# Row maxima of an attention kernel turned on VectorE and put in order through DRAM, in place of a product with the identity on TensorE

## The chip, the cores and the metric

The kernel runs on one core of one Trainium2 chip. The metric is the time of one execution on the device in microseconds (us), as the median of several runs; a time below the median before is faster. The profile comes from one further execution, which has its own time.

## The reference

The input x has 2048 rows of 512. Two attention layers of 32 heads with 16 dimensions each work on it, and a gate mixes them. A is full softmax attention over all 2048 keys. B cuts the rows into four segments of 512, takes causal softmax attention inside each segment, and adds what a running memory of the earlier segments gives.

```python
def _A_ref(x, wqkv, wo):
    ...
    scores = jnp.einsum("bhqd,bhkd->bhqk", q, k) * scale
    p = _softmax(scores, axis=-1)
    o = jnp.einsum("bhqk,bhkd->bhqd", p, v)
    ...
def _B_ref(x, wq, wk, wv, wo, beta):
    ...
    for s in range(N):
        ...
        logits = jnp.einsum("bhqd,bhkd->bhqk", qs, ks) * scale + mask
        p = _softmax(logits, axis=-1)
        a_dot = jnp.einsum("bhqk,bhkd->bhqd", p, vs)
        ...
        num = jnp.einsum("bhld,bhde->bhle", pq, M)
        den = jnp.einsum("bhld,bhd->bhl", pq, z)[..., None] + 1e-6
        o = g * (num / den) + (1.0 - g) * a_dot
        ...
g = _sigmoid((x * gate_w).sum(-1, keepdims=True))
return g * a + (1 - g) * b
```

What matters here is the softmax: the kernel needs the maximum of every row of scores before it can take the exponentials of that row.

## The kernel before

**Units and slots.** The work on the scores is cut into units. A unit is one side (A or B), one group g of four heads, and one chunk c of 512 queries. There are 32 units of each side, called k = 0 to 31 in the text (g = k mod 8, c = k div 8). An A unit has 64 slots and a B unit 10; a slot is one bank (128 x 512) of scores. The units follow each other as A0, B0, A1, B1, ..., A30, B30, B31, A31, so one k is 74 slots and there are 2368 slots, `nS`. The main loop counts them as `n`.

**Two passes.** Each score is computed twice. The pass for the maxima runs `LEAD` = 96 slots ahead, at position `m = n + LEAD`: TensorE makes scores with 128 queries in the partitions (`max_product`), and VectorE takes the maximum over the keys of each row, `tensor_reduce` for A, and `tensor_tensor_reduce` with the causal mask for B (`max_part`, `masked`). Four banks hold these scores; TensorE fills them in the order in which VectorE has read them. The first 96 positions run inside the projections (`some_max`). The second pass (`score_part`) makes the scores with the keys in the partitions, and here the maximum must already be subtracted: the query tile `qt[u]` has two further rows, 48 and 49 of each half, which hold the negated maximum in a high and a low part, and the key tiles have ones in these rows. ScalarE then takes the exponential straight from the bank (L805, L808), and TensorE multiplies by the values (`some_values`, L152 by way of the helper `matmul`).

**The order of the work.** It is written by hand. In a slot the jobs booked by `at` come first, then the score, then the part of the maxima, then `run_todo`. Slots come in bursts of three; at the end of a burst TensorE takes values, and in the last 94 slots (`wide`) in every second burst, along with pieces of the closing products (`fill`). `wait_early` puts the waits for loads of the next burst on the last product of the burst before. SyncE issues nearly all DMAs, in program order; a DMA that has to wait for something holds all that stand behind it. Keys and queries are loaded `PRE` = 20 slots ahead. `octet` divides a group of outputs by its sums of exponentials: GpSimd computes the factors, which go to DRAM and come back spread over the partitions; its jobs are booked at fixed distances, and it is put off where its factors would stand ahead of the maxima of a unit on GpSimd.

**The maxima on their way to the query tile.** The maxima of a unit lie as 128 partitions (queries of a block) x 16 (four heads, four blocks of queries). The score pass needs them as two rows of 2 x 512, one per half of the heads. So after the last maximum of a unit, `finish_max` reduces A's four values per row to one on VectorE (L204), and GpSimd splits the 16 columns into high and low part (L208, L209). Up to nine positions later (`LATE_T`) and at the end of a burst, `transpose_max` takes up to two units: TensorE multiplies each by the identity into a bank of the scores (L217), ScalarE copies the bank to `mt` (L220), and SyncE sends four pieces from there into the rows 48 and 49 of the query tiles (L223). A burst that does this does no `fill`.

Of the kernel before, what the change touches and what calls it, by code (L numbers as in the profile page):

```python
# [41 lines left out]
LATE_T = 9  # L42
# [5 lines left out]
def gated_mix(ctx, tc, x, xT, wqkv, a_wo, b_wq, b_wk, b_wv, b_wo, beta, gate_w, out):  # L48
# [88 lines left out]
    def raw(t):  # L137

        return t[:].bitcast(F32)
# [58 lines left out]
    late = []  # L198

    def finish_max(u):  # L200
        nm = pmt.pop(u)
        if u[0] == "A":
            pm, nm = nm, mp.tile([128, 4, 4], F32, tag="nm", name="nm")
            nc.vector.tensor_reduce(nm, pm, axis=AX.X, op=ALU.max, negate=True)  # L204

        ms = mp.tile([128, 2, 2, 2, 4], F32R, tag="ms", name="ms")
        nv = nm.rearrange("p (r h) s -> p r h s", r=2)
        nc.gpsimd.tensor_copy(ms[:, :, 0], nv)  # L208
        nc.gpsimd.tensor_sub(ms[:, :, 1], nv, ms[:, :, 0].bitcast(F32))  # L209
        return ms  # L210

    def transpose_max(us, pool, tag):

        w = 32 * len(us)
        pt = pool.tile([128, CH], F32, tag=tag, name="mt_ps")
        for i, (_, u, ms) in enumerate(us):
            nc.tensor.matmul(pt[32 * i:32 * i + 32, :128], ms.rearrange("p r a h s -> p (r a h s)").bitcast(F32), identf,  # L217
                             start=True, stop=True, tile_position=(0, 32 * i))
        mt = mp.tile([64, 128], F32R, tag="mt", name="mt")
        nc.scalar.copy(mt[:w], pt[:w, :128])  # L220
        for i, (_, u, ms) in enumerate(us):
            for r in range(2):
                lands["score", u, r] = [nc.sync.dma_start(raw(qt[u])[64 * r + 48:64 * r + 50],  # L223
                                                          raw(mt)[32 * i + 16 * r:32 * i + 16 * r + 16])]
# [23 lines left out]
    def max_part(m, bank, b=None):  # L248
# [3 lines left out]
        if u not in pmt:  # L252
            pmt[u] = mp.tile([128, 4, 4] + [4] * (side == "A"), F32, tag="pm" + side, name="pm")
# [29 lines left out]
        if m == last_max[u]:  # L283
            def finish():

                due = min(e for e in a_last if e >= last_max[u]) + LATE_T
                late.append((min(due, first[u] + LEAD - 12), u, finish_max(u)))
            todo.append((m + 1, finish))

    def run_todo(m):  # L290

        for e in [e for e in todo if e[0] <= m]:
            todo.remove(e)
            e[1]()
# [849 lines left out]
```

## Time and profile before

| | |
|---|---|
| median of 3 runs | 1768.63 us (1768.51 to 1768.84) |
| the profiled execution | 1769.23 us, of which its span is 1767.5 us |
| granted clock of TensorE | 1.00 |
| TensorE busy | 1760.7 us, 14873 products |
| VectorE busy | 1564.4 us, 3331 instructions |
| ScalarE busy | 1436.3 us, 2752 instructions |
| GpSimd busy | 641.0 us, 748 instructions |
| DMA | 261.54 MB, mean 148 GB/s |

The span runs from the first to the last instruction. In the rows PE is TensorE, PEld its weight loads, DVE VectorE, ACT ScalarE, POOL GpSimd and SPq the queue of SyncE; L260 is line 260 of the kernel before. The projections take the first 304 us or so, the main loop the rest. The ends of products are modelled, so that busy time of TensorE can hold waiting.

### The profile page before, as it was taken

How to read it: one execution, taken by the hardware profiler on the slowest of the kernel's cores; microseconds unless marked ns; L12 is line 12 of the kernel's file. 1: busy time of each engine (PE TensorE's matmuls, PEld its weight loads, DVE VectorE, ACT ScalarE, POOL GpSimd, SP SyncE). 2: the span in 40 equal slices, each digit the busy share in tenths (PEclk: the TensorE clock that was granted, in tenths of full speed). 3: DMA queues.
4: the chain of work that ended last, by engine and by line, in shares of the span. 5: the costliest groups of instructions: out<-in, count | busy, mean ns of one | idle time of the engine just before them, and what ended most of it. 6: DMA issues, size and time to landing. Idle time of an engine off the chain costs nothing.

```text
span 1767.5 us, 40472 instructions
## 1 busy us (share of the span) xinstructions
PE 1760.7 (100%) x14873; PEld 908.9 (51%) x14873; DVE 1564.4 (89%) x3331; ACT 1436.3 (81%) x2752; POOL 641.0 (36%) x748
## 2 busy tenths in 40 slices
PE   9999999999999999999999999999999999999999
PEld 8887776544444444444444444444444444444444
DVE  4235777999999999999999999999999999999931
ACT  5455444888888888888888888888889888888884
POOL 3002222415161416443434343343434253435343
PEclk9999999999999999999999999999999999999999
DMA  7677556444463436555444544454545444545542
GB/s 246 215 225 249 185 202 192 127 110 136 112 169 107 137 115 183 146 140 136 132 138 126 146 129 147 129 146 115 160 111 158 115 138 118 152 120 139 144 161 62
DMA packets 141269, 261.54 MB, mean 148 GB/s; under 512 B 36328, under 2 KB 58888, under 8 KB 140560
## 3 DMA queue, kind: packets, MB, share of 16 engines
q1 hardware_dynamic: 139712, 257.55, 50.3%
q8 instruction: 118, 1.93, 0.5%
q0 software_dynamic: 1216, 1.14, 0.3%
q14 instruction: 79, 0.65, 0.1%
q10 hardware_dynamic: 144, 0.26, 0.1%
HBM read 174.39 MB, written 83.25 MB: 146 GB/s over the span
## 4 chain that ended last, share of the span: by engine, by line
PE 96%; DVE 1%; ACT 1%; DMA 1%; POOL 1%; issue 0%; SPq 0%; POOLq 0%; ACTq 0%
PE ops L152 40%; PE st L785 27%; PE sm L227 14%; PE pr L352 10%; PE sm L152 2%; PE num L555 1%; POOL mn L419 1%; PE pr L442 1%; PE mps L586 0%; DMA qdB<-q 0%; PE mt_ps L217 0%; DMA raw<-xT 0%; PE sm L785 0%; DVE jk L514 0%; ACT ex L426 0%; DVE pm L260 0%
## 5 line engine op out<-in xcount | busy, mean ns | idle before, releaser
L808 ACT ACTIVATE p<-st 128x512 f32<-128x512 f32 x2261 | 1190.6, 601 | 146.7 <-PE sm L227 88.9
L260 DVE TENSOR_REDUCE pm<-sm 128x1 f32<-128x512 f32 x2048 | 1276.7, 680 | 11.3 <-PE sm L227 11.2
L227 PE MATMUL sm<-kA,qA 48*128 48x512 f32 x2048 | 664.1, 425 | 0.2
L785 PE MATMUL st<-qA,kA 50*128 50x512 f32 x2014 | 656.2, 431 | 0.0
L152 PE MATMUL ops<-p,vA 128*17 128x256 f32 (+3 forms) x6360 | 552.2, 445 | 0.0
L785 PEld LDWEIGHTS st<-qA,kA 50*128 50x128 f32 x2014 | 326.9, 185 | 423.0 <-ACT p L808 380.3
L227 PEld LDWEIGHTS sm<-kA,qA 48*128 48x128 f32 x2048 | 338.0, 185 | 13.1 <-issue 4.2
L904 POOL TENSOR_TENSOR rcp<-rec,minus 128x32 f32<-128x32 f32 x43 | 234.2, 5446 | 79.4 <-DMA rec<-dend 74.9
L275 DVE CUSTOM_DVE_ANT_0 rest<-sm,mask 128x128 f32<-128x128 f32 (+3 forms) x512 | 245.0, 479 | 0.0
L152 PEld LDWEIGHTS ops<-p,vA 128*17 128x17 f32 x6360 | 129.1, 96 | 213.0 <-issue 182.5
L789 POOL TENSOR_SCALAR_AFFINE_SELECT p<-p 128x512 f32<-128x512 f32 x128 | 79.4, 637 | 316.1 <-ACT p L808 311.4
L227 PE MATMUL sm<-kB,qB 48*128 48x128 f32 (+3 forms) x512 | 166.1, 384 | 0.0
L785 PE MATMUL st<-qB,kB 50*128 50x512 f32 (+1 forms) x495 | 105.5, 330 | 0.3 <-ACT mt L220 0.3
L422 DVE TENSOR_TENSOR q<-full,q 128x512 fp32r<-128x512 f32 x56 | 38.4, 688 | 75.5 <-ACT q L415 69.1
L785 PEld LDWEIGHTS st<-qB,kB 50*128 50x128 f32 x495 | 68.6, 186 | 62.0 <-ACT p L808 50.4
L152 PE MATMUL ops<-p,vB 128*17 128x128 f32 (+3 forms) x1504 | 88.4, 350 | 0.0
L227 PEld LDWEIGHTS sm<-kB,qB 48*128 48x128 f32 x512 | 80.0, 184 | 0.0
L208 POOL CAST ms<-nm 128x16 fp32r<-128x16 f32 x32 | 6.3, 196 | 196.7 <-DVE nm L204 194.9
L419 POOL TENSOR_SCALAR mn<-full 128x512 f32<-128x512 f32 x24 | 36.4, 1515 | 102.3 <-ACT full L414 81.9
L414 ACT COPY full<-pr 128x512 f32<-128x512 f32 x56 | 32.8, 587 | 41.1 <-PE pr L352 37.5
L208 POOL CAST ms<-pm 128x16 fp32r<-128x16 f32 x32 | 6.3, 196 | 128.7 <-DVE pm L275 128.6
L920 POOL TENSOR_TENSOR v<-v,inv 128x512 f32<-128x512 f32 x31 | 39.8, 1285 | 26.1 <-DMA inv<-rdA 22.5
(198 smaller groups left out, 1615.6 us busy)
## 6 DMA issues: line engine op xcount, KB each, us to landing
kA<-kdA SPq DMA_DIRECT2D x256, 128.0 KB
vA<-vdA SPq DMA_DIRECT2D x31, 544.0 KB
kA<-kdA SPq DMA_DIRECT2D x256, 64.0 KB
kdA<-q SPq DMA_DIRECT2D x32, 256.0 KB
qdB<-q SPq DMA_DIRECT2D x32, 256.0 KB
qA<-qdA SPq DMA_DIRECT2D x64, 128.0 KB
kdB<-q SPq DMA_DIRECT2D x32, 256.0 KB
qB<-qdB SPq DMA_DIRECT2D x64, 128.0 KB
```

The source lines that it names most:

```text
L152: behind[0] = nc.tensor.matmul(*args, **kw)
L227: nc.tensor.matmul(ps[:, n0:n0 + n], rows(qt[u][:, :, s * 128:(s + 1) * 128], h, 48), rows(k[:, :, k0:k0 + n], h, 48), start=True, stop=True)
L260: nc.vector.tensor_reduce(pm[:, h, s, kc:kc + 1], ps, axis=AX.X, op=ALU.max)
L275: nc.vector.tensor_tensor_reduce(out=tri["rest"][:, 0:w], in0=ps[:, n0:n0 + w], in1=tri["mask"][:, CH - w:], scale=-1.0, scalar=3.0e38, op ...
L352: nc.tensor.matmul(ps, l(a, k), r(b, k), start=(n == 0), stop=(n == 11))
L419: nc.gpsimd.tensor_scalar_min(ph["mn"], full, 0.0)
L422: nc.vector.tensor_sub(q2, full, q1.bitcast(F32))
L785: nc.tensor.matmul(ps[:, n0:n0 + CH - q0], rows(k[:, :, b * 128:(b + 1) * 128], h, 50), rows(q[:, :, q0:], h, 50), start=True, stop=True)
L789: nc.gpsimd.affine_select(out=x, in_=x, pattern=[[0, 4], [1, 128]], base=0, channel_multiplier=-1, compare_op=ALU.is_ge, fill=0.0)
L808: nc.scalar.activation(p[:, h], ps, AF.Exp, scale=SCALE)
L904: eng.tensor_tensor(r, rec, minus, op=ALU.pow)
L920: eng.tensor_mul(k["v"], k["v"], k["inv"])
```

## The change

The maxima of one A unit and one B unit share a tile. `couple` says which: A k goes with B k-1; A0 and B30 are alone, and A31 goes with B31. The tile `nm` has 128 partitions x 32 columns (two units, four heads, four blocks); B's masked maxima are written into it directly, and A's by the reduction as before. When both units of a tile are finished, `turn_max` has VectorE transpose the tile in 32-by-32 blocks, one position after that reduction; GpSimd splits the 32 columns into high and low part once. In the turned tile each block of 32 partitions holds 32 rows (unit, head, block of queries) of 32 queries, so that the pieces of one row lie in four places. SyncE puts them in order through DRAM: `keep_max`, four positions after the turn, stores the high and the low part in `sdm`, in pieces of 128 bytes; `send_max`, ten positions after the turn, loads two rows of 1024 into each half of both query tiles. The product, the copy by ScalarE, the bank, `LATE_T` and the lists `late` and `run_late` are gone; `fill` is no longer left out in any burst, and `octet` is put off by up to two positions more. A tile with one unit is cleared by GpSimd first.

```diff
--- before.py
+++ after.py
@@ -39,7 +39,7 @@
 LOW = 3
 NP = 6
 GAP = {"A": 2, "B": 5}
-LATE_T = 9
+SENT = 4, 10
 PRE = 20
 NKA, NKB = 8, 2
 
@@ -195,33 +195,59 @@
     pmt = {}
     tri = {}
     todo = []
-    late = []
-
-    def finish_max(u):
-        nm = pmt.pop(u)
+
+
+    couple = {}
+    for k in range(NU):
+        couple[unit("A", k)] = (k, 0)
+        if 0 < k < NU - 1:
+            couple[unit("B", k - 1)] = (k, 1)
+    couple[unit("B", NU - 2)] = (NU, 1)
+    couple[unit("B", NU - 1)] = (NU - 1, 1)
+    wanted = {}
+    for u, (k, _) in couple.items():
+        wanted.setdefault(k, set()).add(u)
+    nms = {}
+    sdm = [dr.tile([2, 2, 2, 8, CH // 4], F32, name=f"sdm{i}") for i in range(2)]
+
+    def nm_half(u):
+        k, i = couple[u]
+        if k not in nms:
+            nms[k] = mp.tile([128, 2, 4, 4], F32, tag="nm", name="nm")
+            if len(wanted[k]) == 1:
+                nc.gpsimd.memset(nms[k], 0.0)
+        return nms[k][:, i]
+
+    def finish_max(u, m):
         if u[0] == "A":
-            pm, nm = nm, mp.tile([128, 4, 4], F32, tag="nm", name="nm")
-            nc.vector.tensor_reduce(nm, pm, axis=AX.X, op=ALU.max, negate=True)
-
-        ms = mp.tile([128, 2, 2, 2, 4], F32R, tag="ms", name="ms")
-        nv = nm.rearrange("p (r h) s -> p r h s", r=2)
-        nc.gpsimd.tensor_copy(ms[:, :, 0], nv)
-        nc.gpsimd.tensor_sub(ms[:, :, 1], nv, ms[:, :, 0].bitcast(F32))
-        return ms
-
-    def transpose_max(us, pool, tag):
-
-        w = 32 * len(us)
-        pt = pool.tile([128, CH], F32, tag=tag, name="mt_ps")
-        for i, (_, u, ms) in enumerate(us):
-            nc.tensor.matmul(pt[32 * i:32 * i + 32, :128], ms.rearrange("p r a h s -> p (r a h s)").bitcast(F32), identf,
-                             start=True, stop=True, tile_position=(0, 32 * i))
-        mt = mp.tile([64, 128], F32R, tag="mt", name="mt")
-        nc.scalar.copy(mt[:w], pt[:w, :128])
-        for i, (_, u, ms) in enumerate(us):
-            for r in range(2):
-                lands["score", u, r] = [nc.sync.dma_start(raw(qt[u])[64 * r + 48:64 * r + 50],
-                                                          raw(mt)[32 * i + 16 * r:32 * i + 16 * r + 16])]
+            nc.vector.tensor_reduce(nm_half(u), pmt[u], axis=AX.X, op=ALU.max, negate=True)
+        del pmt[u]
+        k = couple[u][0]
+        wanted[k].remove(u)
+        if not wanted[k]:
+            todo.append((m + 2, lambda: turn_max(k, m + 2)))
+
+    def turn_max(k, m):
+
+        tt = mp.tile([128, 32], F32, tag="tt", name="tt")
+        nc.vector.transpose(tt, nms.pop(k).rearrange("p u h s -> p (u h s)"))
+        ms = mp.tile([128, 2, 32], F32R, tag="ms", name="ms")
+        nc.gpsimd.tensor_copy(ms[:, 0], tt)
+        nc.gpsimd.tensor_sub(ms[:, 1], tt, ms[:, 0].bitcast(F32))
+        sd = sdm[k % 2]
+
+        def keep_max():
+            for i in range(2):
+                nc.sync.dma_start(sd[i].rearrange("u r j (b q) -> b (u r j) q", b=4), raw(ms)[:, i])
+        todo.append((m + SENT[0], keep_max))
+        todo.append((m + SENT[1], lambda: send_max(k, sd)))
+
+    def send_max(k, sd):
+        for u, (k_, i) in couple.items():
+            if k_ == k:
+                for r in range(2):
+                    lands["score", u, r] = [nc.sync.dma_start(raw(qt[u])[64 * r + 48:64 * r + 50],
+                                                              sd[:, i, r].rearrange("a j q -> a (j q)"))]
 
     def max_product(ps, u, h, s, n0, n, k, k0=0):
         nc.tensor.matmul(ps[:, n0:n0 + n], rows(qt[u][:, :, s * 128:(s + 1) * 128], h, 48), rows(k[:, :, k0:k0 + n], h, 48),
@@ -250,7 +276,7 @@
         u, (r, i) = maxs[m]
         side, g, c = u
         if u not in pmt:
-            pmt[u] = mp.tile([128, 4, 4] + [4] * (side == "A"), F32, tag="pm" + side, name="pm")
+            pmt[u] = mp.tile([128, 4, 4, 4], F32, tag="pm", name="pm") if side == "A" else nm_half(u)
         pm = pmt[u]
         ps = bank()
         if side == "A":
@@ -281,23 +307,14 @@
                 rows_left.append(lambda h=h, s=s, n0=n0, w=w: masked(h, s, n0, w))
             rows_left.pop(0)()
         if m == last_max[u]:
-            def finish():
-
-                due = min(e for e in a_last if e >= last_max[u]) + LATE_T
-                late.append((min(due, first[u] + LEAD - 12), u, finish_max(u)))
-            todo.append((m + 1, finish))
+            todo.append((m + 1, lambda: finish_max(u, m)))
 
     def run_todo(m):
 
-        for e in [e for e in todo if e[0] <= m]:
-            todo.remove(e)
-            e[1]()
-
-    def run_late(pool, tag, m):
-        while us := [e for e in late if e[0] < m][:2]:
-            for e in us:
-                late.remove(e)
-            transpose_max(us, pool, tag)
+        while due := [e for e in todo if e[0] <= m]:
+            for e in due:
+                todo.remove(e)
+                e[1]()
 
     loaded = [0]
 
@@ -607,7 +624,6 @@
                 max_part(m + i, lambda: me_sm.tile([128, CH], F32, tag="sm", name="sm"))
             run_todo(m + 3)
             mnext[0] += 4
-            run_late(me_ps, "me", mnext[0])
 
         s0 = now[0]
         for n in range(5):
@@ -940,7 +956,7 @@
         ts = (0, 10, 14, 18, 28, 28) if ending else (0, 10, 18, 22, 32, 44) if (o, c) == (2, last) else (0, 10, 25, 29, 42, 54)
         if t0 is not None:
 
-            t0 += max([e + 2 - LEAD - t0 - ts[1] for e in a_last if 0 <= e + 1 - LEAD - t0 - ts[1] < 12], default=0)
+            t0 += max([e + 4 - LEAD - t0 - ts[1] for e in a_last if 0 <= e + 3 - LEAD - t0 - ts[1] < 12], default=0)
         for n, f in zip(ts, (load, factors, send, factor, scale, store)):
             if t0 is None:
                 f()
@@ -1084,15 +1100,11 @@
 
                 for i in range(4):
                     nc.tensor.matmul(ops[:, 128 * i:128 * i + 128], identf, identf, start=True, stop=True)
-            if any(e[0] < m + 1 for e in late):
-                run_late(st_ps, "st", m + 1)
-            else:
-
-                for _ in range(0 if n >= nS and queue else 4 if n not in wide else 11 - taken if taken < 8 else 0):
-                    if filled[0] == len(fill) or fill[filled[0]][0] > n:
-                        break
-                    fill[filled[0]][1]()
-                    filled[0] += 1
+            for _ in range(0 if n >= nS and queue else 4 if n not in wide else 11 - taken if taken < 8 else 0):
+                if filled[0] == len(fill) or fill[filled[0]][0] > n:
+                    break
+                fill[filled[0]][1]()
+                filled[0] += 1
             if 5 < n < nS:
                 wait_early(n)
         n += 1
```

## The prediction

> **What bounds the kernel now.** I read the page first (engine totals and the slices of the span), then the groups of VectorE for the long middle stage, then the busy time by stretches, then the order of time on VectorE, TensorE and SyncE around one turn of the maxima.
>
> ```profile
> span 1767.5 us, 40472 instructions
> ...
> PE 1760.7 (100%) x14873; PEld 908.9 (51%) x14873; DVE 1564.4 (89%) x3331; ACT 1436.3 (81%) x2752; POOL 641.0 (36%) x748
> ...
> DVE  4235777999999999999999999999999999999931
> ```
>
> By the page TensorE is the bound: 100% busy, 96% of the chain. But ends of matmuls are modelled, so a TensorE that waits for a bank can look busy. VectorE has only 89%, and its slices say why: low in the first seven slices and the last two, nine tenths or more in all the others. So the second view is VectorE alone from 305 to 1650 us, grouped (count | busy, mean ns | idle before).
>
> ```profile
> L260 DVE TENSOR_REDUCE pm<-sm 128x1 f32<-128x512 f32 x1904 | 1185.6, 680 | 0.0
> L275 DVE CUSTOM_DVE_ANT_0 rest<-sm,mask 128x128 f32<-128x128 f32 x480 | 229.6, 478 | 0.0
> ...
> L204 DVE TENSOR_REDUCE nm<-pm 128x16 f32<-128x64 f32 x30 | 6.2, 206 | 0.0
> ```
>
> No group has any idle time before it in 1345 us: VectorE works through the row maxima without a visible pause, and each k (one A unit and one B unit, 74 slots) takes what its maxima take. The stretches (TensorE, weight load, VectorE, ScalarE, GpSimd, then clock and DMA) show three k of that stage and the two stretches at the end:
>
> ```profile
> 614.69:750.25 135.56, 135.56 (x1277) 62.06 (x1278) 135.56 (x292) 120.98 (x235) 58.67 (x70) 1.00 0.54 150
> ...
> 1650.00:1705.00 55.00, 54.70 (x470) 25.19 (x458) 43.30 (x115) 47.74 (x95) 27.56 (x32) 1.00 0.38 112
> 1705.00:1767.00 62.00, 58.56 (x375) 31.32 (x373) 6.73 (x13) 38.79 (x78) 21.99 (x21) 1.00 0.38 123
> ```
>
> In the middle 135.56 of 135.56 us are VectorE's, while ScalarE has 14.6 us to spare. After 1650 VectorE runs out of maxima and TensorE (58.56 of the last 62.00) sets the end. Is VectorE really the one that is late in the middle, or do both run level? The order of time on VectorE answers (start, length):
>
> ```profile
> 592.82 9.49 DVE L260 TENSOR_REDUCE pm<-sm 128x1 f32<-128x512 f32 x15
> 602.22 0.21 DVE L204 TENSOR_REDUCE nm<-pm 128x16 f32<-128x64 f32 x1
> 602.35 3.07 DVE L260 TENSOR_REDUCE pm<-sm 128x1 f32<-128x512 f32 x5
> 605.34 0.28 DVE L275 CUSTOM_DVE_ANT_0 rest<-sm,mask 128x128 f32<-128x128 f32 x1
> ...
> 605.54 0.68 DVE L260 TENSOR_REDUCE pm<-sm 128x1 f32<-128x512 f32 x1
> 606.14 0.54 DVE L275 CUSTOM_DVE_ANT_0 rest<-sm,mask 128x384 f32<-128x384 f32 x1
> ...
> 606.62 0.68 DVE L260 TENSOR_REDUCE pm<-sm 128x1 f32<-128x512 f32 x1
> ```
>
> Five reductions from 602.35 to 605.34 are 0.598 us each, start to start, though each lasts 0.68: they overlap, and 0.60 is VectorE's own pace. The fifteen from 592.82 to 602.22 take 0.627: here TensorE is late, by 15 x 0.029 = 0.44 us. Another is seen 949 us on, 21 k later:
>
> ```profile
> 1541.65 9.49 DVE L260 TENSOR_REDUCE pm<-sm 128x1 f32<-128x512 f32 x15
> ```
>
> So TensorE is at times late, by some tenths of a microsecond in a k that takes 45.2; everywhere else VectorE is the bound, and only what is added to or taken from VectorE moves the end of the stage.
>
> **What is removed.** Per k, a pair of products with the identity on TensorE, a copy by ScalarE, one bank of the scores.
>
> ```profile
> 605.56 0.84 PE L152 MATMUL ops<-p,vA 128*17 128x128 f32 x16
> 606.23 0.39 PE L217 MATMUL mt_ps<-identf,ms 128*32 128x128 f32 x4
> 606.54 0.50 PE L785 MATMUL st<-qA,kA 50*128 50x512 f32 x1
> ...
> 607.50 0.84 PE L152 MATMUL ops<-p,vA 128*17 128x256 f32 x16
> 608.27 0.50 PE L785 MATMUL st<-qA,kA 50*128 50x512 f32 x1
> ```
>
> Without a turn the next scores start 0.77 us after such a group of values (607.50 to 608.27); with it 0.98 (605.56 to 606.54). So a turn costs TensorE 0.21 us. In the middle stage, which holds 30 of the 33, this is hidden: VectorE reduces on from its banks while TensorE does it, and the rows above show no gap at 606. I cost that removal at nothing there; if TensorE were the bound it would be 0.21 us each (rival below). The copy by ScalarE lies in ScalarE's spare time, and the bank likewise: nobody waits for them in the middle.
>
> Two places have no such cover. In the projections, where TensorE leads, and after the last maxima:
>
> ```profile
> 275.91 0.41 PE L217 MATMUL mt_ps<-identf,ms 128*32 128x128 f32 x2
> 276.25 1.13 PE L555 MATMUL num<-ph,mbd 128*128 128x512 f32 x2
> ```
> ```profile
> 1697.71 1.91 PE L152 MATMUL ops<-p,vA 128*17 128x512 f32 x16
> 1699.44 0.39 PE L217 MATMUL mt_ps<-identf,ms 128*32 128x128 f32 x4
> 1699.76 0.50 PE L785 MATMUL st<-qB,kB 50*128 50x512 f32 x2
> 1700.56 0.44 PE L785 MATMUL st<-qB,kB 50*128 50x384 f32 x1 [0.30 <-ACT mt L220]
> ```
>
> The first gives 276.25 - 275.91 = 0.34 us. The last turn takes 0.32 (1699.44 to 1699.76), and then the third score waits for the bank until the copy is done: the row shows 0.30 of it as idle. With the other late turn, taken at 0.21 as in the middle, the end gains 0.83 us. Bounds: nothing, if another wait ends last there, and 2.85 us (all of 1697.71 to 1700.56) at most. Taken: 0.34 + 0.83 = 1.2 us.
>
> **What is added on VectorE.** One turn of 128 x 32 per k: of 33 one falls into the projections, one (k = 31) behind the last maximum, and 31 into VectorE's full stage. The trace has no such instruction. Nearest rows: the masked pass over 128 columns takes 0.20 us to the next start (605.34 to 605.54), over 384 columns 0.48 (606.14 to 606.62): 0.0011 per column and 0.06 fixed. The 64-column reduction agrees (602.22 to 602.35, 0.13). [...] The lower bound is the fixed part alone, 0.06. The upper bound is the widest spacing of a small VectorE instruction that I find:
>
> ```profile
> 264.45 0.28 DVE L595 TENSOR_TENSOR mrun<-mps,mrun 128x136 f32<-128x136 f32 x1
> 264.77 0.46 DVE L596 SCALAR_TENSOR_TENSOR mbd<-mrun,gh,bmask 128x128 f32<-128x128 f32 x1
> ```
>
> 0.32 us, where the second waits for the first's result. The 64-column row is nearest, so 0.13: 31 x 0.13 = 4.0 us, with 31 x 0.06 = 1.9 and 31 x 0.32 = 9.9 as ends. The turn reads what the L204 reduction left one slot before; one maximum of 0.60 us lies between, so that result is there.
>
> [...]
>
> **GpSimd and SyncE.** GpSimd splits once per k instead of twice, 32 columns instead of 16.
>
> ```profile
> 602.50 0.20 POOL L208 CAST ms<-nm 128x16 fp32r<-128x16 f32 x1 [9.04 <-DVE nm L204]
> 602.77 0.22 POOL L209 TENSOR_TENSOR ms<-nm,ms 128x16 fp32r<-128x16 f32 x1
> ...
> 1655.94 0.64 POOL L789 TENSOR_SCALAR_AFFINE_SELECT p<-p 128x512 f32<-128x512 f32 x1 [12.74 <-ACT p L808]
> ```
>
> It waits for the maxima (9.04 us here), so it is there at once; behind its wait stand the factors of an octet, which the change moves two slots (1.2 us) back, with the loads and stores of that octet on SyncE, off the end's path. Two memsets are new, for the k with one unit; the second falls before 1655.94, into 12.74 us in which GpSimd only waits. Cost nothing, 0.3 us if VectorE had to wait for one.
>
> SyncE gets two stores and then loads that wait for both stores' landing; behind that wait are key loads, issued 20 slots (12 us) ahead. The old send was also waited for there. The B unit's first score is who would notice:
>
> ```profile
> 1243.65 0.37 SPq L913 DMA_DIRECT2D rdB<-rec  x1
> ...
> 1248.30 0.58 SPq L917 DMA_DIRECT2D inv<-rdB  x1
> ```
> ```profile
> 608.44 1.26 SPq L223 DMA_DIRECT2D qA<-mt  x2
> ```
> ```profile
> 613.73 0.49 PE L785 MATMUL st<-qA,kA 50*128 50x512 f32 x1
> 614.07 0.63 PE L785 MATMUL st<-qB,kB 50*128 50x512 f32 x2
> ```
>
> The store and load of the octet's factors, of the same shape, show a store's round trip of up to 4.65 us (1243.65 to 1248.30, SyncE waiting). For this k: turn at 602.95 (one maximum after L204), split done 603.8, second store issued about 604.0, landed by 608.65 at worst; then four loads, 0.63 us of issue each (608.44, two in 1.26) and A's ahead of B's, the last starting at 610.55. The rows must be there before 613.73. That leaves 3.2 us for the load to land, or 7.8 us for both landings. I cost it at nothing.
>
> [...]
>
> **The sum.** 4.0 - 1.2 = +2.8 us. The profiled execution took 1769.23 us (span 1767.5 and 1.7 around it) and becomes 1772.0; the median of the runs lies 0.6 lower, 1768.63, and becomes 1771.4.
>
> **Rivals.**
> - The turn does not overlap its neighbours on VectorE. Each reduction now starts the next 0.08 us before its own end (0.68 against 0.60); if reordering empties the pipe, a turn costs 0.2 to 0.32 us, 31 of them 6.2 to 9.9, the sum +5.0 to +8.7: 1773.6 to 1777.3, slower. It decides from 0.15 us a turn (31 x 0.15 - 1.2 = 3.5). For it: a reordering is unlike any row here. Against: every other form overlaps. [...]
> - The score rows come late: both landings over 7.8 us. TensorE then stands, VectorE lives an estimated 1.2 us on its filled banks (two maxima), and the rest is lost. With 4.65 us for each landing the rows are 1.5 us late, 0.3 lost in each of 30 k: 9 us on top of the 2.8, 1780.4 us, slower. For it: the round trip and A's loads ahead of B's. Against: a small load is read by one or two descriptors and the queues are half idle (0.54).
> - TensorE is the bound after all: then 30 x 0.21 = 6.3 us come back, with the 1.2: 1761.1, faster. For it: the page's 100% and the late stretches. Against: VectorE's even 0.598 and its idle 0.0.
> - The cheap end: 1.9 added, up to 3.2 won at both uncovered places: 1767.3.
>
> **How the numbers follow.** About 0.2% (3.5 us) is what a measurement here can tell from no change. Forecast with a turn of 0.09 to 0.15 us, 0.49 (all within 0.2%); cheap end 0.09 (within, but for 0.01 faster); no overlap 0.27; late rows 0.06; TensorE bound 0.09. So faster 0.10, same 0.57, slower 0.33. The range goes from the cheap end (1767.3, widened to 1767.0) to the dearest turn with only 0.5 us won: 1768.6 + 9.9 - 0.5 = 1778.0; TensorE as the bound and late rows, 0.15, are left out.
>
> **What would show it.** Right: VectorE's groups still have idle 0.0 from 305 to 1650, a new group of 31 turns with about 0.13 us to the next start, three k take 135.56 + 3 x 0.13 = 135.95 us; no row of TensorE waits for a load into qB; 275.91 and 1699.44 close up. Wrong: three k in less than 135.5 us (TensorE was the bound), spacing over 0.16, or scores of a B unit waiting for a DMA.

## The result: slower by 0.45%, inside the range and above the forecast

The kernel after takes 1777.16 us in the median (1772.88 to 1780.91, six runs) against 1768.81 (1768.51 to 1769.35); the ratio is 1.0045, 95% interval 1.0035 to 1.0055. That is +8.4 us where +2.8 was forecast. The runs also spread over 8.0 us, against 0.84 before. The execution that the profile shows is one of the short ones: 1775.33 us, +6.1 on the profiled execution of before.

The head of the page after:

```profile
span 1773.6 us, 40153 instructions
...
PE 1762.3 (99%) x14745; PEld 914.8 (52%) x14745; DVE 1567.9 (88%) x3364; ACT 1429.9 (81%) x2719; POOL 631.0 (36%) x688
```

TensorE is at 99% now. The turn itself is there as forecast. VectorE's groups from 305 to 1650 us, and the order of time around the turn of the k shown before:

```profile
L286 DVE TENSOR_REDUCE pm<-sm 128x1 f32<-128x512 f32 x1897 | 1183.2, 680 | 0.0
...
L233 DVE STREAM_TRANSPOSE tt<-nm 128x32 f32<-128x32 f32 x30 | 6.0, 199 | 0.0
```
```profile
602.32 0.21 DVE L223 TENSOR_REDUCE nm<-pm 128x16 f32<-128x64 f32 x1
602.44 0.68 DVE L286 TENSOR_REDUCE pm<-sm 128x1 f32<-128x512 f32 x1
603.04 0.20 DVE L233 STREAM_TRANSPOSE tt<-nm 128x32 f32<-128x32 f32 x1
603.16 2.44 DVE L286 TENSOR_REDUCE pm<-sm 128x1 f32<-128x512 f32 x4
```

The turn lasts 199 ns and the next reduction starts about 0.12 us after the turn's start (603.04 to 603.16); it overlaps its neighbours like the other forms around it. So the price of one turn, 0.13, was right. What was not forecast is in the waits of TensorE, 305 to 1670 us, and of VectorE, 305 to 1650 (total, times, longest):

```profile
PE ops L152 <- DMA qB<-sdm: 3.5, 2, 1.8
```
```profile
DVE rest L301 <- PE sm L253: 1.7, 1, 1.7
```

Twice TensorE stands until a load into qB has landed: B's score rows come late. The first time is at 705 us (the second falls behind 1650):

```profile
702.48 1.05 PE L152 MATMUL ops<-p,vA 128*17 128x384 f32 x14
705.25 0.38 PE L152 MATMUL ops<-p,vA 128*17 128x128 f32 x2 [1.72 <-DMA qB<-sdm]
```

SyncE's order of time shows why. First the k around 603 us, where the rows are in time, then the one that is late at 705 (its turn is at 693.28):

```profile
603.54 1.26 SPq L241 DMA_DIRECT2D sdm<-ms  x2
606.26 0.53 SPq L249 DMA_DIRECT2D qA<-sdm  x2
606.85 0.54 SPq L249 DMA_DIRECT2D qB<-sdm  x2
```
```profile
693.37 0.53 SPq L186 DMA_DIRECT2D kA<-kdA  x1
...
696.34 0.47 SPq L754 DMA_DIRECT2D vA<-vdA  x1
697.15 1.30 SPq L241 DMA_DIRECT2D sdm<-ms  x2
702.62 0.56 SPq L249 DMA_DIRECT2D qA<-sdm  x2
703.23 0.54 SPq L249 DMA_DIRECT2D qB<-sdm  x2
```

At 603 the stores go out half a microsecond after the turn, and the loads follow 2.7 us behind (603.54 to 606.26). At 697 seven loads are issued first (from 693.37 to 696.34, keys, output blocks and values), and then the stores take 5.5 us until the loads may go (697.15 to 702.62), because they travel behind those big loads: in the trace the packets of the blocks and values move from 696.6 to 701.4 and the 128-byte pieces of the stores from 700.6 to 702.0. The load into qB is issued at 703.23 and lands two microseconds later, at 705.2.

The second late row, at 1657.81, is late mainly in the queue. Its turn is at 1645.94, but two of B's key loads stand ahead of the stores and wait, one 2.1 us for the blocks to land, the other 2.4 us for the values:

```profile
1651.84 0.30 SPq L187 DMA_DIRECT2D kB<-kdB  x1
1652.24 1.59 SPq L241 DMA_DIRECT2D sdm<-ms  x2
1655.29 0.53 SPq L249 DMA_DIRECT2D qA<-sdm  x2
```

Here the loads follow the stores after only 3.1 us. From the turn to the first load it is 9.3 us in both late k. A long landing alone does no harm: in the k whose turn is at 1102.60 the stores leave at 1103.11, the loads follow 5.9 us behind them, and no row is late.

How much of the 6.1 us is what? A mark that returns in every k is A's last reduction; from its row in k = 1 to its row in k = 30 are 29 k. Before, then after:

```profile
331.14 0.21 DVE L204 TENSOR_REDUCE nm<-pm 128x16 f32<-128x64 f32 x1
...
1641.19 0.21 DVE L204 TENSOR_REDUCE nm<-pm 128x16 f32<-128x64 f32 x1
```
```profile
330.71 0.20 DVE L223 TENSOR_REDUCE nm<-pm 128x16 f32<-128x64 f32 x1
...
1645.21 0.21 DVE L223 TENSOR_REDUCE nm<-pm 128x16 f32<-128x64 f32 x1
```

The 29 k take 1310.05 before and 1314.50 after, 4.45 more. One of them, the late one, took 47.50 us where the others of its kind take 45.54: 1.96. The other 2.5 are the turns, 0.09 in each k. The last k, with the second late row, is 2.05 longer (53.85 for 51.80). The stage starts 0.43 earlier (331.14 to 330.71). 4.45 + 2.05 - 0.43 = 6.07, and the end, which was to gain 0.83, gives nothing. The rows of the end that answer to 1697.71, 1699.76 and 1700.56 of before:

```profile
1703.56 1.91 PE L152 MATMUL ops<-p,vA 128*17 128x512 f32 x16
1705.40 0.68 PE L801 MATMUL st<-qB,kB 50*128 50x512 f32 x3
1705.74 0.34 PE L801 MATMUL sm<-qB,kB 50*128 50x384 f32 x1
```

From the values to the score that had to wait for the bank, it is 2.18 us now and was 2.85: 0.67 are won here, of which 0.4 are left at the next product of values (1701.28 before, 1706.72 after). The other late turn gives 0.2, so that TensorE gains 0.6 in all. It is lost at the very end. ScalarE's last copy of the result, before and after:

```profile
1763.60 0.58 ACT L1107 COPY res<-sm 128x512 f32<-128x512 f32 x1 [0.72 <-PE sm L152]
```
```profile
1769.02 0.58 ACT L1119 COPY res<-sm 128x512 f32<-128x512 f32 x1 [0.72 <-PE sm L152]
```

From there to the end of the span are 3.9 us before (1767.5 - 1763.60) and 4.6 after (1773.6 - 1769.02): what stands behind the last copy took 0.7 longer. It isn't the landing of the last stores: in the trace SyncE's last wait for one ends at 1766.6 before and at 1771.9 after, 0.9 and 1.7 us from the end, so that the 0.7 lie in the program's closing instructions. In the kernels below the stretch from the last copy is 3.8 to 4.3 us; such a difference of one profile each is taken as scatter. In the kernel below that has no product it is 3.9 as before, and there the 0.6 is seen: from the last maximum to the end it is 74.5 us, for 75.1 before.

### The profile page after: what moved, and what is told of

It is laid out like the page before. It is cut to its first block, busy times and chain, and to the rows that moved or that the text cites. A ratio compares the mean times of both kernels' runs of the same rounds, so it can differ in the third digit from the quotient of the medians.

```text
span 1773.6 us, 40153 instructions
## 1 busy us (share of the span) xinstructions
PE 1762.3 (99%) x14745; PEld 914.8 (52%) x14745; DVE 1567.9 (88%) x3364; ACT 1429.9 (81%) x2719; POOL 631.0 (36%) x688
## 3 DMA queue, kind: packets, MB, share of 16 engines
q0 software_dynamic: 1216, 1.14, 0.3%
## 4 chain that ended last, share of the span: by engine, by line
PE 92%; DMA 3%; DVE 1%; ACT 1%; POOL 1%; issue 0%; SPq 0%; POOLq 0%; ACTq 0%; DVEq 0%
PE ops L152 39%; PE st L801 26%; PE sm L253 14%; PE pr L369 9%; PE sm L152 2%; POOL mn L436 1%; PE pr L459 1%; PE num L572 1%; DVE pm L286 1%; DMA vA<-vdA 0%; DMA qdB<-q 0%; DMA kA<-kdA 0%; ACT full L431 0%; DMA sdm<-ms 0%; PE sm L801 0%
## 5 line engine op out<-in xcount | busy, mean ns | idle before, releaser
L253 PE MATMUL sm<-kA,qA 48*128 48x512 f32 x2048 | 672.7, 428 | 0.3
L235 POOL CAST ms<-tt 128x32 fp32r<-128x32 f32 x33 | 6.9, 210 | 234.8 <-DVE tt L233 234.7
L152 PEld LDWEIGHTS ops<-p,vB 128*17 128x17 f32 x1504 | 33.6, 96 | 27.9 <-issue 24.2
```

The costliest lines, as they stand in the source:

```text
L152: behind[0] = nc.tensor.matmul(*args, **kw)
L253: nc.tensor.matmul(ps[:, n0:n0 + n], rows(qt[u][:, :, s * 128:(s + 1) * 128], h, 48), rows(k[:, :, k0:k0 + n], h, 48), start=True, stop=True)
```

## The experiments

The theory behind the forecast was that VectorE alone is the bound in the middle, so that a turn there costs its 0.125 us, TensorE's relief nothing, and SyncE and GpSimd nothing. The rivals: TensorE is (also) the bound, and the score rows come late through SyncE's queue and the two trips through DRAM. For each kernel the time of the 29 k is read as above; where GpSimd does A's last reduction, from the reductions behind it, which serve as marks in the same way. Two more stretches are named below: the projections, from A1's first reduction to A2's first (64.16 us before, 64.05 after), which holds their end, and the last k, from A30's last reduction to the end of A31's last (51.80 before).

**The turn alone.** The kernel before, with one turn of a constant tile per k on VectorE.

```diff
+    blank = const.tile([128, 32], F32, name="blank")
+    nc.gpsimd.memset(blank, 0.0)
+
+    def dead_turn():
+        tt = mp.tile([128, 32], F32, tag="tt", name="tt")
+        nc.vector.transpose(tt, blank)
...
             todo.append((m + 1, finish))
+            if u[0] == "A":
+                todo.append((m + 2, dead_turn))
```

> The kernel before, with one more VectorE instruction per k: a transpose of a constant 128 x 32 tile one position after A's last reduction, whose result nobody reads. Products, copies and sends stay. Theory (VectorE is the bound of the middle stage, a turn costs 0.125 us to the next start): 30 turns in the full stage, +3.8 us, about 1772.5, with no spread between runs. Rival (the turn itself is free or hidden, and all that the change lost it lost in waits for the score rows): 1768.7, within 0.5 us of the kernel before. Rival (a turn empties the pipe): +6 or more.

Measured: 1771.7 us (1770.68 to 1772.59), ratio 1.0014 (1.0006 to 1.0023), +2.9 us.

```profile
331.60 0.21 DVE L210 TENSOR_REDUCE nm<-pm 128x16 f32<-128x64 f32 x1
...
1644.45 0.21 DVE L210 TENSOR_REDUCE nm<-pm 128x16 f32<-128x64 f32 x1
```

1312.85, which is 2.80 over before and 0.097 per k: about three quarters of a turn's 0.125 stay. That is the forecast's main term, by itself. The runs lie within 1.9 us, so the turn makes neither the rest of the loss nor the spread.

**The product twice.** The kernel before, with both products with the identity done a second time.

```diff
-        for i, (_, u, ms) in enumerate(us):
+        for i, (_, u, ms) in [e for e in enumerate(us) for _ in range(2)]:
```

> The kernel before, with every product that turns the maxima done twice into the same bank (the second overwrites the first). Theory (TensorE's 0.21 us per turn is hidden behind VectorE in the middle stage): only the places without that cover show it, +0.3 in the projections and at most 0.6 at the end, so under +1 us. Rival (TensorE is as much the bound as VectorE): 30 x 0.2 = +6 us and more.

Measured: 1775.18 us, ratio 1.0034 (1.0022 to 1.0047), +6.3 us. The expectation failed.

```profile
330.20 0.21 DVE L204 TENSOR_REDUCE nm<-pm 128x16 f32<-128x64 f32 x1
...
1645.88 0.21 DVE L204 TENSOR_REDUCE nm<-pm 128x16 f32<-128x64 f32 x1
```

1315.68: 5.63 more, 0.19 per k. The second pair takes 0.24 us of TensorE (from the values to the scores it is now 1.22 us, for 0.98 before), so four fifths of it stay. TensorE has next to no margin in the middle.

**No product.** The kernel before without product, copy and bank: the rows are sent straight from ms, in the wrong order.

```diff
-        pt = pool.tile([128, CH], F32, tag=tag, name="mt_ps")
...
-        nc.scalar.copy(mt[:w], pt[:w, :128])
...
-                                  raw(mt)[32 * i + 16 * r:32 * i + 16 * r + 16])]
+                                  ms.rearrange("p r a h s -> p (r a h s)").bitcast(F32)[64 * r:64 * r + 64])]
```

> The kernel before without the product, the copy by ScalarE and the bank: the rows 48 and 49 are filled straight from the split maxima, in the wrong order, by the same number of sends at the same places; no turn on VectorE and no way through DRAM. It shows what the removal alone is worth. Theory: the two places without cover, 0.4 in the projections and 0 to 0.8 at the end, so 1767.5 to 1768.4. Rival (TensorE the bound): 1761 to 1762.

Measured: 1768.21 us, ratio 0.9996 (0.9987 to 1.0004). The 29 k take 1310.08, as before (1310.05). So taking 0.21 away gives nothing, though adding 0.24 costs most of it.

**A's last reduction on GpSimd.** The kernel before, with 0.125 us per k taken from VectorE.

```diff
-            nc.vector.tensor_reduce(nm, pm, axis=AX.X, op=ALU.max, negate=True)
+            d = mp.tile([128, 4, 4, 3], F32, tag="d", name="d")
+
+            def larger(out, a, b):
+                nc.gpsimd.tensor_sub(out, a, b)
+                nc.gpsimd.tensor_scalar_max(out, out, 0.0)
+                nc.gpsimd.tensor_add(out, out, b)
+            larger(d[:, :, :, 0:2], pm[:, :, :, 0:2], pm[:, :, :, 2:4])
+            larger(d[:, :, :, 2:3], d[:, :, :, 0:1], d[:, :, :, 1:2])
+            nc.gpsimd.tensor_scalar_mul(nm, d[:, :, :, 2], -1.0)
```

> The kernel before with A's last reduction (four values per row to one, 0.126 us on VectorE per k) made by seven small GpSimd instructions instead, as b + max(a - b, 0) twice and a change of sign. Theory (VectorE is the bound): 30 x 0.126 = -3.8 us, about 1765.0, since GpSimd has some 9 us of waiting ahead of these maxima and the product that needs them comes up to nine positions later. Rival (both engines run level, so that taking from VectorE alone gives nothing): 1768.7. Rival (the later split delays the product or the sends): slower.

Measured: 1768.25 us, ratio 0.9997 (0.9988 to 1.0006). The expectation failed: the 29 k take 1309.55, half a microsecond less, where VectorE as the only bound had to give 29 x 0.125 = 3.6. Two of every three k became shorter by 0.08 (44.96 to 44.88, 45.10 to 45.03), the third longer by 0.13 (45.46 to 45.59); why the third grows isn't shown.

**Both at once.** The two last edits together (the rows in the wrong order again).

> The kernel before with both removals at once: no product, copy and bank (rows sent straight from the split maxima, in the wrong order), and A's last reduction on GpSimd. Alone each gave -0.6 us. Theory (VectorE and TensorE run level, so that what is taken from one is waited for at the other): together more than the sum, in the middle stage some 0.1 us per k, about 1765.5. Rival (VectorE alone is the bound and some third thing limits it): the sum of the two, 1767.6.

Measured: 1765.13 us, ratio 0.9973 (0.9962 to 0.9983), -4.3 us.

```profile
328.77 2.49 DVE L261 TENSOR_REDUCE pm<-sm 128x1 f32<-128x512 f32 x4
...
1635.85 2.48 DVE L261 TENSOR_REDUCE pm<-sm 128x1 f32<-128x512 f32 x4
```

1307.08: 2.97 less, where the two edits alone gave 0.0 and 0.5. So the two engines run level in the middle. To take from one alone gives next to nothing, because the other is right behind; to add to either costs most of what is added; to take from both pays.

**Rows without the round trip.** The kernel after, its stores kept, but the rows loaded from a DRAM tile that is filled once, so that no load waits for a store (the rows are not the maxima then).

```diff
+    fixed = dr.tile([2, 2, 2, 8, CH // 4], F32, name="fixed")
...
-        todo.append((m + SENT[1], lambda: send_max(k, sd)))
+        todo.append((m + SENT[1], lambda: send_max(k, fixed)))
```

> The changed kernel with its stores as they are, but with the rows loaded from another DRAM tile that is filled once at the start, so that no load waits for the landing of a store (the rows are not the maxima). Theory: SyncE no longer stands between store and load, 2.2 to 5 us are gone from the way, and no row is late: about 1771.5. Rival (SyncE's backlog of issues ahead of the stores, or the loads' own landing, makes the rows late): waits for qB remain, over 1773.

Measured: 1771.22 us (1770.51 to 1772.40), ratio 1.0009 (1.0000 to 1.0018). No wait for qB is left, the 29 k take 1312.79, and the time is that of the turn alone. What the change costs beyond its turn, and its spread, hangs on the load's wait for the store.

**Everything as early as it can be.** The kernel after with no slots of delay before the stores and loads, and B's rows ahead of A's.

```diff
-SENT = 4, 10
+SENT = 0, 0
...
-        for u, (k_, i) in couple.items():
+        for u, (k_, i) in reversed(couple.items()):
```

> The changed kernel with the two stores and the loads of the rows right behind the turn in SyncE's order (SENT 0, 0 in place of 4, 10), so ahead of the value tile (544 KB) and the blocks (512 KB) that are issued one slot later, and with B's rows ahead of A's. Theory (the changed kernel's cost above the turn's 2.9 us comes from rows of B that land late, because their stores and loads stand behind those big loads): no wait of TensorE for a load into qB, little spread, about 1771.5. Rival (the way through DRAM is late by itself, whatever stands ahead): waits as before, 1774 to 1780. Rival (SyncE, held earlier at the landing of the stores, delays other loads): slower than the changed kernel, with TensorE waiting for keys or values.

Measured: 1782.05 us, ratio 1.0068 (1.0055 to 1.0080), slower still. In the 29 k no row is late (1312.86, as with the turn alone), but the projections got 5.8 us longer (69.85 for 64.05), and the last k 6.6 (58.5 for 51.9). In the last k SyncE is held at the new stores (5.3 us, until GpSimd's split is done), and a key load behind them comes late. TensorE's waits from 1650 us on, and the stretches around (in the order of the prediction's), the first of them in the projections:

```profile
PE ops L152 <- DMA kB<-kdB: 3.2, 1, 3.2
```
```profile
282.70:289.50 6.80, 6.80 (x13) 4.14 (x14) 4.74 (x11) 1.08 (x2) 0.00 (x0) 0.50 0.91 202
...
1664.00:1668.00 4.00, 2.55 (x9) 1.17 (x9) 0.13 (x1) 0.35 (x1) 0.00 (x0) 0.64 0.39 121
1668.00:1670.00 2.00, 2.00 (x12) 0.15 (x8) 1.93 (x6) 1.27 (x3) 0.65 (x1) 0.50 0.00 0
1670.00:1672.00 2.00, 2.00 (x14) 1.46 (x10) 0.56 (x3) 1.36 (x3) 0.00 (x0) 0.51 0.02 7
1672.00:1674.00 2.00, 2.00 (x16) 1.38 (x14) 1.96 (x7) 1.30 (x3) 0.00 (x0) 1.00 0.36 132
```

The stall of 3.2 us is followed by a granted clock of about one half until 1672, which loses another 4 x 0.36 + 2 x 0.50 + 2 x 0.49 = 3.4 us. With the 3.2 that is the 6.6 of the last k: this stall cost twice what its wait shows. In the projections the clock is one half for 6.8 us as well, which is 3.4 of the 5.8.

**Stores from GpSimd.** The kernel after with the stores issued by GpSimd right behind its split, loads as they were.

```diff
-SENT = 4, 10
+SENT = 0, 10
...
-                nc.sync.dma_start(sd[i].rearrange("u r j (b q) -> b (u r j) q", b=4), raw(ms)[:, i])
+                nc.gpsimd.dma_start(sd[i].rearrange("u r j (b q) -> b (u r j) q", b=4), raw(ms)[:, i])
```

> The changed kernel with the two stores issued by GpSimd, right behind its split, on its own queue; the loads stay on SyncE ten positions after the turn. Theory (the stores are late because of SyncE's order and the one queue): GpSimd issues them about 1 us after the turn, SyncE finds them landed, no late rows: 1771.5 to 1772.5. Rival (GpSimd's queue takes longer to land, or its issue holds back the factors behind it): more late rows, or GpSimd's pow later, 1775 and more.

Measured: 1773.7 us (1772.78 to 1775.71), ratio 1.0023 (1.0015 to 1.0032).

TensorE's wait for qB, and SyncE's from 516 to 525 us:

```profile
PE ops L152 <- DMA qB<-sdm: 1.2, 1, 1.2
```
```profile
SPq L249 <- DMA sdm<-ms: 7.1, 1, 7.1
```

Two k are still late, by less (46.02 for 45.05, and 53.2 for 51.9 in the last; the wait shown is that of the last), and the projections take 2.6 us longer, of which 1.7 are a granted clock of one half from 276.9 to 280.3. Half a cure: the store leaves early, but that doesn't make it land early. In the first of the two k the stores are issued at 515.87, 0.2 us after a load of values, and SyncE stands 7.1 us at the loads until they have landed. In the last k the loads stand behind the waiting key loads, as in the kernel after, and then wait 2.9 us more.

**Early only where nothing is in the way.** The kernel after with no delay for 0 < k < 30 and the old delays elsewhere, and with B's rows first in every k.

```diff
+        sent = (0, 0) if 0 < k < 30 else SENT
...
-        for u, (k_, i) in couple.items():
+        for u, (k_, i) in reversed(couple.items()):
```

> The kernel after, with the stores and loads of the score rows both put ahead of the big key and value loads (no slots of delay, B's rows first) for every k of the middle stage, and left where they were in the two k whose early store stood in the way of loads (the first one, in the projections, and the last ones). If the late rows of B and SyncE's stand behind a store are what the change costs beyond its turn, no k of the middle has a late row, and the time falls from 1777 us to that of the dead turn alone, 1771.7, plus at most 1.9 for the late row that k = 30 keeps: 1771.5 to 1773.5. If the excess came from something else that the new turn brings (GpSimd's one long split, the missing score bank, the moved octet factors), it stays at 1775 or above.

Measured: 1771.11 us (1770.48 to 1772.48), ratio 1.0012 (1.0004 to 1.0021). No wait for qB or for keys up to 1670 us.

```profile
330.54 0.20 DVE L223 TENSOR_REDUCE nm<-pm 128x16 f32<-128x64 f32 x1
...
1643.19 0.20 DVE L223 TENSOR_REDUCE nm<-pm 128x16 f32<-128x64 f32 x1
```

1312.65, again the time of the turn alone. All that it changes is the place of six DMAs in SyncE's queue. So the loss of the change is settled in two parts: 2 to 3 us for the turn, and the rest for late rows. In k = 30, where the old delays stand, this profile has no late row either: the stores leave 3.4 us after their turn (1643.91 to 1647.26) instead of 6.3, because the key loads ahead of them waited less. How much of that is owed to the edit isn't shown.

**The same, with A's last reduction on GpSimd.** The turn comes three slots later, and VectorE's work per k is that of the kernel before again.

```diff
-            nc.vector.tensor_reduce(nm_half(u), pmt[u], axis=AX.X, op=ALU.max, negate=True)
...
+            nc.gpsimd.tensor_scalar_mul(nm_half(u), d[:, :, :, 2], -1.0)
...
-            todo.append((m + 2, lambda: turn_max(k, m + 2)))
+            todo.append((m + 5, lambda: turn_max(k, m + 5)))
```

> As the kernel before it in this list, and A's last reduction (64 columns, 0.125 us on VectorE) done by GpSimd in seven short operations, the turn three slots later. VectorE then has the same work per k as in the kernel before (a turn for a reduction), and TensorE 0.21 us less. If both engines run level, the middle stage is that of the kernel before or 0.1 us per k shorter, and the time 1766 to 1770 us. If VectorE had margin for the turn and only late rows counted, the time is that of the list's first kernel, 1771.5 to 1773.5.

Measured: 1858.0 us, ratio 1.0499 (1.0484 to 1.0513); neither expectation. TensorE's waits, and GpSimd's order of time in one late k:

```profile
PE ops L152 <- DMA qB<-sdm: 46.5, 13, 5.6
```
```profile
424.88 0.27 POOL L231 TENSOR_SCALAR nm<-d 128x16 f32<-128x16 f32 x1
425.10 5.46 POOL L929 TENSOR_TENSOR rcp<-rec,minus 128x32 f32<-128x32 f32 x1
...
432.30 0.21 POOL L243 CAST ms<-tt 128x32 fp32r<-128x32 f32 x1
```

Between the reduction and the split, GpSimd now has an octet's reciprocal, 5.46 us, and five more steps of it; the split comes 7.2 us after the reduction. The edit had moved the split past the slots that the change keeps free of octets.

The 13 stalls are 46.5 us of the 89 that are lost. After 11 of them the granted clock was one half, for 3.4 or 6.8 us each, which loses another 27. Whether it falls isn't settled by the length of the stall alone: behind two stalls of 1.9 us, which end at 825.37 and at 1399.12, are these stretches:

```profile
825.50:829.00 3.50, 3.50 (x25) 1.39 (x23) 2.11 (x7) 2.15 (x5) 0.00 (x0) 1.00 0.77 260
...
1400.80:1404.20 3.40, 3.40 (x18) 1.36 (x16) 2.26 (x7) 2.43 (x5) 0.00 (x0) 0.50 0.43 115
```

**The octets put off.** The last kernel, with every octet step within six slots of A's last maximum behind the turn.

```diff
-            t0 += max([e + 4 - LEAD - t0 - ts[1] for e in a_last if 0 <= e + 3 - LEAD - t0 - ts[1] < 12], default=0)
+            t0 += max([e + 7 - LEAD - t0 - ts[1] for e in a_last if 0 <= e + 6 - LEAD - t0 - ts[1] < 12], default=0)
...
+        if n < nS - 90 and any(0 <= n + LEAD - e < 6 for e in a_last):
+            beside[n + 1] = beside.pop(n, []) + beside.get(n + 1, [])
```

> The kernel with the early rows and A's last reduction on GpSimd, once more, now with every step of an octet that falls within six slots after A's last maximum put off behind the turn on GpSimd's queue, so that the 5.46 us reciprocal no longer stands between the reduction and the split (in the run before it did, and the rows came up to 8 us late). The k without such a collision took 44.92 to 44.94, 45.08 and 45.44 us there, against 44.96, 45.10 and 45.46 in the kernel before. If that reading is right, no k has a late row and the middle (k = 2 to 30) takes 1309.1 us, 3.5 less than with the turn and the reduction both on VectorE; with the 0.6 gained in the projections and 0.4 at the end: 1767 to 1768. If VectorE had room for the turn, the time stays at the 1771 of the kernel with early rows. If rows sent 1.8 us later (three slots) are late again, scores of B wait for qB and the time is 1770 or above.

Measured: 1769.35 us (1768.80 to 1771.56), ratio 1.0005 (0.9996 to 1.0014).

```profile
330.12 2.47 DVE L295 TENSOR_REDUCE pm<-sm 128x1 f32<-128x512 f32 x4
...
1638.97 2.47 DVE L295 TENSOR_REDUCE pm<-sm 128x1 f32<-128x512 f32 x4
```

1308.85, against 1309.1 expected: no late row, VectorE with the work that it had before, TensorE with 0.21 less, and 0.04 per k gained on before. The 1.2 us that this wins in the middle are lost in the projections (65.38 for 64.16), and the 1767 to 1768 expected for the whole were missed. Level with the kernel before, not better.

**A little from both.** The kernel before with A's last reduction on GpSimd and the two products made one, from one tile with both units' maxima.

```diff
...
+            nc.tensor.matmul(pt[0:64, :128], us[0][2][0].rearrange("p u r a h s -> p (u r a h s)").bitcast(F32), identf,
+                             start=True, stop=True)
...
```

> The kernel before with a little taken from both engines, nothing left out: A's last reduction goes to GpSimd (0.125 us per k off VectorE) and the two products with the identity become one, from one tile that holds both units' maxima (half of the 0.21 us per k off TensorE). If VectorE and TensorE run level, taking 0.1 from both shortens each k by 0.05 to 0.1 us: 1765.5 to 1767.5. If VectorE alone is the bound in the middle, the time is that of the moved reduction alone, 1768.2 or less by nothing; if TensorE alone is, 30 x 0.1 = 3 us come off, 1765.8, which the moved reduction's own result (no gain) speaks neither for nor against.

Measured: 1773.41 us, ratio 1.0022 (1.0013 to 1.0031). It was to be the version that beats both kernels, and it is slower than before. TensorE's order of time:

```profile
607.10 0.84 PE L152 MATMUL ops<-p,vA 128*17 128x128 f32 x16
607.88 0.43 PE L235 MATMUL mt_ps<-identf,ms 128*64 128x128 f32 x2
608.24 0.49 PE L806 MATMUL st<-qA,kA 50*128 50x512 f32 x1
```

From the values to the scores are 1.14 us, where it was 0.98 with the two products and 0.77 without: one product of 64 columns costs 0.37 us, two of 32 columns 0.21. So this kernel took 0.125 from VectorE and added 0.16 to TensorE. Read so, it agrees with the level engines: its k are 0.13 to 0.16 longer than with the moved reduction alone (45.04, 45.19 and 45.72 in the mean, for 44.89, 45.03 and 45.60). Why one product of 64 columns costs 0.16 more than two of 32 isn't shown here.

## Why the prediction was right where it was, and where it failed

- **The turn on VectorE: right.** 0.13 us was taken, as for the reduction of 64 columns; about 0.125 was measured, and the dead turn alone gives +2.9 us where 4.0 was summed. That a quarter of it doesn't show in the 29 k would fit the stretches in which TensorE was late anyway, but no run shows it. The first rival (the turn empties VectorE's pipe, 0.27) is out: the turn is 199 ns long and the next instruction starts after 0.12, before its end, and the upper price of 0.32 was 2.5 times too high.
- **"Only what is added to or taken from VectorE moves the end of the stage": wrong.** This was read from VectorE's idle 0.0 and its even 0.598. Those rows show that VectorE has no pause; they don't show that TensorE has slack. The second pair of products cost 5.6 us in the 29 k, and the reduction taken from VectorE gave 0.5. The rows for it stood in the prediction: the fifteen reductions at 0.627 are stretches in which TensorE is late.
- **The removal of the product at nothing: right in its number, not in its reason.** The 29 k stay at 1310.1 without it. But it is not hidden under spare time of TensorE; VectorE's own load is right behind. The rival "TensorE is the bound after all" (1761.1) failed by the same run.
- **SyncE and GpSimd at nothing: the step that failed.** The bound was worked out there (7.8 us for both landings), and the store and load were held against one round trip of 4.65 us at the ideal time of issue. What it left out: the stores' place in SyncE's queue (they left 3.9 and 6.3 us after the turn in the two late k, rather than half a microsecond), and that the loads ahead are big and the store lands behind them (5.5 us until the loads may go, in the first of the two). That a row load is small is so: the four of the second late k are eight packets of 4 KB, 0.03 MB in all (1656.0 to 1657.3). But "the queues are half idle (0.54)" is a mean over 135 us and says nothing of the microseconds behind a burst.
- **The rival "score rows come late" (0.06) was the right mechanism at the wrong size.** It had 0.3 us lost in each of 30 k; it is 1.96 and 2.05 in two of 32 in the profiled execution. Its cushion failed too: VectorE was to live 1.2 us on its banks, so that 0.3 of 1.5 is lost. TensorE stood 1.7 and the k grew by 1.96: with the engines level there is no speed with which to catch up.
- **The gain at the end, 0.83: 0.6 on TensorE, but not seen in the time**, since the program's closing instructions took 0.7 longer in the profiled execution. The stage starts 0.43 earlier where 0.34 was forecast, but that is luck: 0.31 of it is there before the product that is removed (A0's last reduction starts at 268.77 before and at 268.46 after), so that 0.12 stands against the 0.34.
- **The sum**: forecast +4.0 - 1.2 = +2.8; profiled +2.5 (turns in the 29 k) + 1.96 + 2.05 (late rows, of which about 0.1 is a turn) - 0.43 + 0.0 = +6.1. Without late rows, in the kernel with the rows sent early in the middle, it is +2.0 on the kernel before (1771.11 for 1769.14), close to the +2.8 of the forecast. The range held by luck: its upper end was drawn for the dearest turn, which did not come, and late rows were left out of it.
- **The spread**: the median is 1.8 us above the profiled run, and single runs reach 1780.9. Only two of the six runs had a mean clock of 1.0, the shortest two; the others had 0.997 to 0.999. Each span times its mean clock gives 1771.2 to 1773.9 (to about 1 us, as the clock is given to 0.001), so that the 8.0 us of spread shrink to 2.7: the longer runs lost their time to a lower clock. The kernels whose rows are not late don't show it (1.9 us of spread without the wait for the store, 2.0 with the rows sent early in the middle). That a late row's stall sets off the lower clock fits the kernel with A's reduction on GpSimd, where one of the two stalls of 1.9 us shown did and the other did not, but no such run of the kernel after was profiled; that step stays open.

## What to carry to other kernels

An engine without a pause need not be the only bound: before an edit on a neighbour is costed at nothing, look for stretches in which that neighbour is late, since two level engines gave next to nothing here when one was relieved (0.0 and 0.5 us in the 29 k) and charged about four fifths when either was loaded (0.097 of 0.125 us per k on VectorE, 0.19 of 0.24 on TensorE). A small transfer pair through DRAM is costed from its place in the issuing queue and from the big loads just ahead of it (2.7 us from issue to issue at 603 us, 5.5 behind such loads at 697), not from the mean share of the queues, and moving six small DMAs ahead of a burst was worth more here (6.0 us, 1777.16 to 1771.11) than all the arithmetic that the change moved (2.9 us for the turn). Where such an early transfer is itself waited for, check what stands behind it in the queue, at the ends of the program above all (5.8 us were lost in the projections and 6.6 in the last k when all rows were sent early).

## What the runs showed of the hardware

- A 32-column turn on VectorE of 128 partitions of four-byte data takes 199 ns, and the next instruction starts 0.12 us after its start.
- A stall of TensorE of 3.2 us was followed by a granted clock of one half, up to 1672 us. Of the two stalls of 1.9 us shown for the kernel with A's reduction on GpSimd one was (0.50 from 1400.8 to 1404.2) and one was not (1.00 from 825.5 to 829.0); the stalls of 1.7 and 1.8 us in the kernel after were not (1.00 from 705.3 to 712.1 and from 1657.8 to 1664.6). The half clock lasted 3.4 or 6.8 us each time.
- Two fp32 products of 32 columns at different column offsets cost TensorE 0.21 us together, one of 64 columns 0.37.
- The same store and load through DRAM took 2.7 us from issue to issue at 603 us, and 5.5 us behind big loads at 697. Stores issued by GpSimd right behind a load of values held SyncE's load for 7.1 us (from 516.6 to 523.7).
